# Moving the v loads of an attention and gated scan kernel from SyncE's DMA queue to ScalarE's, with all orders searched anew

## The chip, the core and the metric

The kernel runs on one core of a Trainium2 chip. The metric is the device time in microseconds (us) of one execution, as a median over several runs. A run counts as slow when it is over 1.5% above the fastest run of the same kernel in its group; only fast runs enter the ratios. Several kernels below have runs on both sides of that mark, and this is said where it matters. The kernel before itself straddles it in two groups: with v1, v2 and e4 four of its 7 runs count as slow, with e5, v7 and v2's repeat seven of its 11, most of them at a granted clock of 0.99 to 1.00. Ratios from these groups compare with its fastest runs (fast means 174.6 and 173.9 us), so they come out up to 1% high.

## The reference, cut to what matters

```python
scores = q @ k.T / sqrt(64)              # 8 batches, 8 heads, 576 positions, 64 wide
scores = where(|i - j| <= 32, scores, -1e9)
x = softmax(scores) @ v                  # then heads side by side: 8 x 576 x 512
val, gate = split(x @ w_in)              # 512 -> 2 x 512
h[t] = exp(A_log[0]) * h[t-1] + val[t]   # a scan over the 576 positions
out = (silu(gate) * h) @ w_out           # 512 -> 512, float32
```

Inputs are float32 and are cast on the chip to half precision.

## The kernel before

The order of every engine's work is fixed in advance: one string per engine holds one letter for each operation (`SEQ`), a second table says which engine takes an operation that several could do (`SHARED`), and `ORDER` lists the loads. A small model in the program replays these strings to give out buffers and to merge them into one program.

```python
SLOTS = {"stg": 5, ..., "v32": 2, "vE": 2, "vO": 2, "pr": 3, ..., "f2k": 16, ...}
SEQ = {
    "act": "qexExhxexwhwwxwwxgegEgxhvxTgkTEgwgegqxooxEgovooeoxxETxxEoeogxgTxxgxegEkvgvxxgeEooxxg"
    ...                                  # cut
    "sp": "LLLLLLLLLLLLLLLLLLLLLLLLLLLLLLLLLLLLLLLLLLLLLLLLLLLLLLLLLLLLLLLLOLLOOLLLOLLLLLLLOOOL"
    ...                                  # cut; L is any load, O a store of the output
}
ORDER = ["q01", "a", "q00", "k00", "v01", "v00", "w00", "k01", "k10", "v02", "v03", "q10",
         "v04", "w01", "w02", "w11", "w03", "w12", "w13", "w10", "q11", "k11", "v10", "v11", ...]
...
        if kd == "ld" and key[0] in "qk":          # rows of 9 x 64 floats: 2304 bytes
            nc.sync.dma_start(out=bf(n, b, T).rearrange("p y j d -> p y (j d)"), in_=...)
        elif kd == "ld" and key[0] == "v":         # rows of 64 floats: 256 bytes
            _, b, x = key
            lo = 128 * x - 32
            p0, p1 = max(0, -lo), min(128, S - lo)
            nc.sync.dma_start(out=bf("v32", b)[p0:p1, x],
                              in_=v[b, :, lo + p0:lo + p1, :].rearrange("h p d -> p h d"))
...                                      # cut
        elif kd == "out":
            nc.sync.dma_start(out=out_flat[r0:r0 + 128, :], in_=bf("o", *key))
    idle = keep_busy(seq, place, 45.0)   # filler matmuls in the first 45 us
```

Names as in the profile: v is the float32 buffer of a v load; vE its cast, vO the copy shifted by 64 positions; pr the exponentials; qT, kT the transposed q and k; f2k a buffer that weights, scans and outputs share. A batch has five v loads: three of 128 positions (1024 rows of 256 bytes, 64 for each of 16 DMA engines) and, at its two ends, two of 96 (48 rows each).

The softmax here doesn't subtract the row's maximum and nothing guards it: scores larger than these inputs give would overflow.

Of the kernel before, what the change touches and what calls it, by code (L numbers as in the profile page):

```python
# [22 lines left out]
    ("act", "ev"): (1.012, 1.18), ("act", "exp"): (0.905, 1.09), ("act", "tanh"): (0.48, 0.63),  # L23
# [13 lines left out]
START = {"pe": 0.5, "act": 2.5, "dve": 0.5, "pool": 5.0, "sp": 0.8}  # L37
SWITCH, CAP, DLAT, DPRE = 0.095, 190, 1.75, 0.65
SLOTS = {"stg": 5, "q16": 2, "k16": 2, "qT": 3, "kT": 3, "v32": 2, "vE": 2, "vO": 2, "pr": 3,
         "rc": 2, "x16": 2, "xT": 2, "f2k": 16, "th": 3, "si": 3, "fu": 2}  # L40
LETTER = {"L": "ld", "w": "cw", "a": "ar", "k": "ck", "K": "trk", "E": "evk", "q": "cq", "Q": "trq",
          "e": "evq", "v": "cv", "h": "sh", "m": "mask", "S": "sc", "x": "exp", "P": "pv", "r":
          "rc", "n": "norm", "t": "xt", "T": "xe", "V": "pjv", "G": "pjg", "s": "scan", "g": "tanh",
          "u": "silu", "f": "fuse", "F": "fin", "o": "fev", "O": "out"}

SEQ = {
    "pe": "mQmQKSKKmSPSQPSmtmPSPSVtVGQGKGmSGPPmVStVPPGVKtGVVQGVSSFFFKGQFFQFmmSPSPKPPtSSFtKQVPPF"
          "GVSGtmmSVSPPVGSQtGKPPGVVSSGQKFVFSSPGFPPtGVQtKFGPSSGQKVFFGQVSSFtPPFVQtGKGPPSVGKVGVFFS"
          "SVGtFPPSFQtKVQVSSPGVGGFKFPPPFtVSSSGtFVGVGSPFFVFVPPPVFtGGVGVtGFVGGVFFFFFFF",
    "act": "qexExhxexwhwwxwwxgegEgxhvxTgkTEgwgegqxooxEgovooeoxxETxxEoeogxgTxxgxegEkvgvxxgeEooxxg"  # L50
           "kqogveEogxvxEgqooegxokxeogEgvxgvgEoxxogToxoeEexxgkgoEovgvoTxxgxoggooxoTggoTgogggoooo"
           "oo",
    "dve": "akaEehkhrnqrnETrnrnssTussuhvhurrnnshsrsrnnsussssusussvusmmqehvhurnrnrnrnqTmmrnrsnhhu"
           "ussrrnnsumTurrnnsushhmusrmmnrunrnTTusrnuhmeushsuTrnrnsTmurnusrunshshmsuurrnnmTssmrsu"
           "unrrnnrunhhsTusmsmrnuusmrnsrrnsunussssuusuussso",
    "pool": "aaqvkvvvvmwwwqkvvvfffqfwwwffkvvkffkvvvvvmqffkfqvvvfvqmfffkvfmvfqmffkkvfvvfmqfqmfvfvm"
            "fvfmffffffffff",
    "sp": "LLLLLLLLLLLLLLLLLLLLLLLLLLLLLLLLLLLLLLLLLLLLLLLLLLLLLLLLLLLLLLLLOLLOOLLLOLLLLLLLOOOL"
          "LLLOOLOLOLOOOLOOOOLOOOOOOOOOOOOOOOOOO",
}  # L60
SHARED = {
    "cw": "GAAAAAGGGGGA",
    "ar": "GDGD",
    "ck": "DGDGAGGGGAAGAGGA",
    "evk": "DADAAAAAAAAAAAAA",
    "cq": "AGDGGADDGGAGAGGG",
    "evq": "ADAAADAAAAADAAAA",
    "cv": "GGGGGGGDGADGAGDGGGGGGAAGGGAGAGGAAGGGAGAG",
    "sh": "DDAADDADDDDDDDDDDDDD",
    "mask": "pppGppppDDppDDGppDDDDGDGGDDGGDDGGDDD",  # L70
    "xe": "DDAAADADDDDDADADAA",
    "fev": "AAAAAAAAAAAAAAAAAAAAAAAAAAAAAAAAADAA",
}
ORDER = ["q01", "a", "q00", "k00", "v01", "v00", "w00", "k01", "k10", "v02", "v03", "q10",
         "v04", "w01", "w02", "w11", "w03", "w12", "w13", "w10", "q11", "k11", "v10", "v11",
         "v12", "v13", "v14", "k20", "q20", "v22", "w23", "w22", "w20", "w21", "v20", "q21",
         "k21", "v21", "q30", "v23", "v24", "k30", "k31", "q31", "v30", "v33", "v31", "v32",
         "v34", "v44", "q40", "k41", "k40", "v41", "q41", "v40", "v42", "v43", "q51", "q50",
         "v50", "v51", "k50", "k51", "v52", "v53", "v63", "q60", "v54", "v60", "k60", "q61",
         "v61", "k70", "v62", "k61", "v71", "v64", "q70", "q71", "v73", "v70", "v72", "k71",  # L80
         "v74"]
# [3 lines left out]
def issue(o):  # L85
    return 0.9 if o.kind == "ld" and o.key[0] == "v" else 0.45


def DESC(o):

    return {"v": 48 if o.key[2:] in ((0,), (4,)) else 64, "q": 16, "k": 16, "w": 8, "a": 32}[o.key[0]] if o.kind == "ld" else 8
# [16 lines left out]
def build(order):  # L108
# [15 lines left out]
    g = last.get  # L124
    for it in order:
        if it[0] in "qk":
            add("ld", it, 0, ("sp",), 1.82, (), [("stg", it)])
        elif it[0] == "v":
            _, b, e = it
            add("ld", it, 0, ("sp",), 1.05 if e in (0, 4) else 1.3, (),  # L130
                [("v32", ("v32", b))])
        elif it[0] == "a":
            add("ld", it, 0, ("sp",), 0.8, ())
        else:
            add("ld", it, 0, ("sp",), 0.79, (), [("f2k", ("w32",) + it[1:])])
    for i in range(3):
        for a in range(4):
            add("cw", (i, a), 0.2 * i + 0.05 * a, ("dve", "act", "pool"), "cw", [g(("ld", "w", i, a))], (), [("w32", i, a)])
    for cc in range(4):
        add("ar", (cc,), 0, ("dve", "pool"), "ar", [g(("ld", "a"))])  # L140
    for b in range(B):
        for T in range(2):
            st = step_of(b, T)
            for n in "kq":
                c = add("c" + n, (b, T), st, ("pool", "dve", "act"), "cqk", [g(("ld", n, b, T))],
                        [(n + "16", (n + "16", b, T))], [(n, b, T)])
                t = add("tr" + n, (b, T), st, ("pe",), "tr", [c], [("ps2", ("tr" + n, b, T))], [(n + "16", b, T)])
                add("ev" + n, (b, T), st, ("act", "dve"), "ev", [t], [(n + "T", (n + "T", b))], [("tr" + n, b, T)])
        for e in range(5):
            add("cv", (b, e), step_of(b, 0) + 0.1 * e, ("pool", "act", "dve"), "cv", [g(("ld", "v", b, e))],  # L150
                [("vE", ("vE", b))], [("v32", b)])
        for T in (0, 1) if b < 2 else (2,):
            es = range(4) if T == 2 else range(2 * T, 2 * T + 2)
            for i in range(2):
                add("sh", (b, T, i), step_of(b, 0) + 0.1 * i, ("dve", "act"), "sh" if T == 2 else "sh1",
                    [g(("cv", b, e + i)) for e in es], [("vO", ("vO", b))], [("vE", b)])
# [22 lines left out]
    for c in range(NCH):  # L179
# [18 lines left out]
        for tt in range(4):  # L198
            k, st = (c, tt), 4 * c + tt
            fs = (2 * (tt // 2), 2 * (tt // 2) + 1) if hv else range(4)  # L200
            f = add("fin", k, st, ("pe",), "fin", [g(("fuse", c, x)) for x in fs] + [g(("cw", 2, a)) for a in range(4)],
                    [("ps1", ("fo",) + k)], [("fu", c)])
            e = add("fev", k, st, ("act", "dve") if c == NCH - 1 else ("act",), "fev", [f], [("f2k", ("o",) + k)], [("fo",) + k])
            add("out", k, st, ("sp",), 0.79, [e], (), [("o",) + k])
# [5 lines left out]
def follow():  # L210
# [4 lines left out]
    eng_of = {"p": "pe", "A": "act", "D": "dve", "G": "pool"}  # L215
# [20 lines left out]
    mode, dma, lock, seq, ring = 0, 2.4, 0.0, [], []  # L236
# [4 lines left out]
    while len(seq) < len(ops):  # L241
        best = None
        for e in ENGINES:
            if not todo[e]:
                continue
            o = todo[e][-1]
            if any(d.end is None for d in o.deps):
                continue
            r = max([d.end for d in o.deps] + [0.0])
            for p, k in o.new:  # L250
                if k in held:
                    continue
                if p == "ps1":
                    c = [t for t in bank if t is not None]
                elif p == "ps2":
                    c = [max(bank[b], bank[b + 1]) for b in pairs()]
                else:
                    c = list(free[p].values())
                r = max(r, min(c)) if c else 1e9
            if r > 1e8:  # L260
                continue
            s = max(r, tf[e])
            if e == "pe" and MODE.get(o.kind, 0) != mode:
                s = max(r, tf[e] + SWITCH)
            if best is None or s < best[0]:
                best = (s, e, o)
        s, e, o = best
        todo[e].pop()
        if e == "sp":
            dma = max(dma, s + issue(o) + DPRE) + o.cost  # L270
            o.end = dma + DLAT
            ring.append((dma, o.cost, DESC(o)))
            room, tf[e] = CAP, s + issue(o)
            for end, took, n in reversed(ring):
                if end <= tf[e]:
                    break
                if n > room:
                    tf[e] = max(tf[e], end - room / n * took)
# [70 lines left out]
def kernel(  # L349
# [40 lines left out]

    for tl in bufs["v32"]:
# [47 lines left out]
    def emit(o):  # L439
# [17 lines left out]
        elif kd == "ld" and key[0] == "v":  # L457
            _, b, x = key
            lo = 128 * x - 32
            p0, p1 = max(0, -lo), min(128, S - lo)  # L460
            nc.sync.dma_start(out=bf("v32", b)[p0:p1, x],
                              in_=v[b, :, lo + p0:lo + p1, :].rearrange("h p d -> p h d"))
        elif kd == "ld" and key[0] == "a":
            nc.sync.dma_start(out=a_log, in_=moe_A_log.rearrange("(a p) -> p a", p=128))
            nc.scalar.activation(a1, a_log, AF.Exp, bias=0.0, scale=1.0)
# [142 lines left out]
        elif kd == "out":  # L608
            c, tt = key
            r0 = 512 * c + 128 * tt  # L610
            nc.sync.dma_start(out=out_flat[r0:r0 + 128, :], in_=bf("o", *key))
# [37 lines left out]
```

## Time and profile before

| | before |
|---|---|
| median of the first 3 runs | 175.71 us (175.24 to 176.26) |
| span of the profiled run, granted clock | 174.8 us, 1.00 |
| busy: TensorE, VectorE, ScalarE, GpSimd | 162.5, 144.6, 130.8, 114.9 us |
| first scores, first projection | 15.24, 28.95 us |

The main views are in the prediction below. Four more lines are needed for the comparison. First, section 4 of the page, the chain that ended last, as shares of the span by engine:

```profile
PE 65%; DVE 13%; ACT 8%; POOL 7%; issue 5%; POOLq 0%; ACTq 0%; DVEq 0%
```

No DMA is on this chain. Next, GpSimd's wait for v loads (us in total, times, longest), and how long a v load takes from issue to landing (shortest, median, longest):

```profile
POOL vE L429 <- DMA v<-in_v_dram: 6.5, 4, 2.2
...
DMA to landing us min/median/max: 3.9/7.2/9.0
```

Last, the stretch from 40 to 50 us (length, then busy time of PE, PEld, DVE, ACT, POOL, the granted clock, the DMA share, GB/s):

```profile
40.00:50.00 10.00, 9.96 (x147) 8.80 (x145) 9.50 (x17) 7.75 (x10) 5.67 (x7) 1.00 1.10 322
```

Both TensorE and the DMA engines are full there.

### The profile page before, as it was taken

What the parts mean: (1) busy time and instruction counts of PE and PEld (TensorE: products, weight loads), DVE (VectorE), ACT (ScalarE), POOL (GpSimd) and SP (SyncE); (2) the same over time, 40 slices, a digit from 0 to 9 for tenths busy, and PEclk for the clock granted to TensorE, in tenths of its full rate; (3) what the DMA queues carried; (4) which work ended last, traced back from release to release, by engine and by line L of the source; (5) the groups of instructions that cost most, each with busy time, mean ns of one, the idle gap of its engine ahead of it and who ended that gap; (6) DMA issues with size and microseconds to landing.
All of it is one profiled execution on the core that took longest, in us unless ns stands there. A gap on an engine that the chain in (4) does not pass through costs nothing.

```text
span 174.8 us, 5309 instructions
## 1 busy us (share of the span) xinstructions
PE 162.5 (93%) x2178; PEld 101.8 (58%) x2178; DVE 144.6 (83%) x233; ACT 130.8 (75%) x172; POOL 114.9 (66%) x117
## 2 busy tenths in 40 slices
PE   1996999979999899999999999999999999999991
PEld 0343657848976585565647655654674654558740
DVE  5348467798999989999998899999979699899850
ACT  2232599886699998869999999877998993545552
POOL 7954409672699393499719879885999855505550
PEclk9999999999999999999999999999999999999999
DMA  4999999899999999999999999999950311401155
GB/s 125 293 294 271 313 373 288 162 326 325 329 208 344 226 219 342 270 245 267 264 307 267 325 303 348 262 323 311 353 174 4 120 64 60 161 23 60 64 212 208
DMA packets 53671, 41.23 MB, mean 236 GB/s; under 512 B 39312, under 2 KB 39312, under 8 KB 53648
## 3 DMA queue, kind: packets, MB, share of 16 engines
q1 hardware_dynamic: 53648, 40.90, 81.5%
q8 instruction: 17, 0.28, 0.7%
q14 instruction: 6, 0.05, 0.1%
HBM read 31.46 MB, written 9.44 MB: 234 GB/s over the span
## 4 chain that ended last, share of the span: by engine, by line
PE 65%; DVE 13%; ACT 8%; POOL 7%; issue 5%; POOLq 0%; ACTq 0%; DVEq 0%
PE psum L576 25%; PE psum L604 14%; PE psum L616 7%; PE psum L493 5%; PE psum L546 4%; PE psum L561 4%; PE psum L522 4%; DVE vO L425 3%; DVE si L589 3%; DVE f2k L584 2%; DVE pr L536 2%; ACT pr L527 2%; POOL fu L599 1%; ACT qT L422 1%; POOL pr L536 1%
## 5 line engine op out<-in xcount | busy, mean ns | idle before, releaser
L576 PE MATMUL psum<-xT,w_in 128*128 128x256 f16 (+1 forms) x384 | 69.9, 326 | 0.0
L576 PEld LDWEIGHTS <-w_in 128*128 128x128 f16 x384 | 35.5, 98 | 20.3 <-issue 0.2
L584 DVE TENSOR_TENSOR_SCAN f2k<-arep,f2k,psum 128x512 f32<-128x512 f32 (+1 forms) x44 | 44.4, 1029 | 1.9 <-PE psum L576 1.3
L527 ACT ACTIVATE pr<-psum 128x1024 f16<-128x1024 f32 x36 | 36.5, 1034 | 7.8 <-PE psum L522 7.4
L599 POOL TENSOR_TENSOR fu<-f2k,si 128x512 f16<-128x512 f32 x24 | 30.0, 1255 | 11.2 <-DVE si L589 7.0
L604 PE MATMUL psum<-w_out,fu 128*128 128x512 f16 x144 | 35.1, 379 | 0.1
L536 POOL TENSOR_TENSOR pr<-pr,mask 128x1024 f16<-128x1024 f16 x9 | 20.0, 2219 | 19.3 <-ACT pr L527 19.3
L587 ACT ACTIVATE th<-psum 128x512 f16<-128x512 f32 x36 | 21.8, 604 | 7.0 <-PE psum L576 6.9
L589 DVE SCALAR_TENSOR_TENSOR si<-th,psum 128x512 f16<-128x512 f16 x36 | 24.1, 676 | 3.0 <-ACT th L587 2.8
L422 ACT ACTIVATE f2k<-psum 128x512 f32<-128x512 f32 x35 | 20.8, 612 | 6.9 <-PE psum L604 6.2
L555 DVE TENSOR_TENSOR x<-psum,rc 128x512 f16<-128x512 f32 x36 | 24.1, 683 | 0.6
L596 POOL TENSOR_TENSOR fu<-f2k,si 128x512 f16<-128x512 f32 x12 | 14.8, 1232 | 13.7 <-DVE f2k L584 6.1
L429 POOL TENSOR_SCALAR vE<-v 128x512 f16<-128x512 f32 x27 | 18.2, 687 | 6.5 <-DMA v<-in_v_dram 6.5
L604 PEld LDWEIGHTS <-fu 128*128 128x128 f16 x144 | 13.2, 98 | 13.5 <-issue 0.2
L422 ACT ACTIVATE qT<-psum 128x1152 f16<-128x1152 f16 x13 | 14.8, 1141 | 3.9 <-PE psum L493 3.7
L422 ACT ACTIVATE kT<-psum 128x1152 f16<-128x1152 f16 x14 | 16.0, 1146 | 1.7 <-PE psum L493 1.7
L546 PEld LDWEIGHTS <-pr 128*64 128x64 f16 x576 | 11.4, 111 | 7.1 <-issue 4.5
L522 PEld LDWEIGHTS <-kT 64*128 64x128 f16 x576 | 10.4, 95 | 8.0 <-issue 4.5
L522 PE MATMUL psum<-qT,kT 64*128 64x64 f16 x576 | 13.5, 191 | 1.7 <-DVE kT L425 1.5
L546 PE MATMUL psum<-vO,pr 128*64 128x65 f16 x256 | 13.4, 197 | 1.7 <-DVE vO L425 1.7
L546 PE MATMUL psum<-vE,pr 128*64 128x65 f16 x320 | 14.0, 197 | 0.3 <-DVE pr L536 0.2
L616 PE MATMUL psum<-eye,ident 128*128 128x512 f16 x44 | 13.7, 457 | 0.4 <-ACT pr L527 0.4
(58 smaller groups left out, 198.7 us busy)
## 6 DMA issues: line engine op xcount, KB each, us to landing
stg<-in_q_dram SPq DMA_DIRECT2D x16, 576.0 KB, 7.2
stg<-in_k_dram SPq DMA_DIRECT2D x16, 576.0 KB, 6.6
out_dram<-f2k SPq DMA_DIRECT2D x36, 256.0 KB, 4.2
v<-in_v_dram SPq DMA_DIRECT2D x24, 256.0 KB, 7.4
v<-in_v_dram SPq DMA_DIRECT2D x16, 192.0 KB, 6.9
f2k<-in_moe_w_in_dram SPq DMA_DIRECT2D x8, 256.0 KB, 7.4
f2k<-in_moe_w_out_dram SPq DMA_DIRECT2D x4, 256.0 KB, 7.6
a_log<-in_moe_A_log_dram SPq DMA_DIRECT2D x1, 2.0 KB, 4.2
```

What stands on the lines that cost most here:

```text
L422: nc.scalar.activation(dst, src, AF.Copy, bias=0.0, scale=mul)
L522: nc.tensor.matmul(out=sc[:, h, 256 * t + 64 * r:256 * t + 64 * r + 64], lhsT=kT[64 * h:64 * h + 64, 64 * i:64 * i + 128], rhs=qT[64 * h:6 ...
L527: nc.scalar.activation(bf("pr", *key), bf("sc", *key), AF.Exp, bias=0.0, scale=1.0 / 8.0)
L536: (nc.vector if e == "dve" else nc.gpsimd).tensor_tensor(out=pr, in0=pr, in1=m[:, None, :].to_broadcast([128, 2, 512]), op=ALU.mult)
L546: nc.tensor.matmul(out=pv[p0:p0 + 64, h, x0:x0 + 65], lhsT=pr[:, h, at:at + 64], rhs=vt, start=True, stop=True)
L555: nc.vector.tensor_tensor(out=x, in0=view[:, :, :, 0:64], in1=bf("rc", *key)[:, :, :, None].to_broadcast([128, 2, 4, 64]), op=ALU.mult)
L576: nc.tensor.matmul(out=to, lhsT=w_in16[:, fc, 128 * w:128 * w + 128], rhs=xT[:, fc, t0:t0 + n], start=(fc == 0), stop=(fc == 3))
L584: nc.vector.tensor_tensor_scan(out=bf("h", c, x)[:, lo:lo + n], data0=arep[:, cc, a0:a0 + n], data1=bf("pjv", c, x)[:, lo:lo + n], initial ...
L589: nc.vector.scalar_tensor_tensor(out=bf("si", *key), in0=bf("th", *key), scalar=1.0, in1=bf("pjg", *key), op0=ALU.add, op1=ALU.mult)
L599: eng.tensor_tensor(out=bf("fu", c)[:, x, :], in0=bf("h", *key), in1=bf("si", *key), op=ALU.mult)
L604: nc.tensor.matmul(out=fo, lhsT=fu[:, cc, 128 * tt:128 * tt + 128], rhs=w_out16[:, cc, :], start=(cc == 0), stop=(cc == 3))
L616: nc.tensor.matmul(out=psum[:, bank, :], lhsT=ident, rhs=eye8.rearrange("p r q -> p (r q)"), start=True, stop=True)
```

## The change

The intent: v loads have short rows and long issues, and they hold up the other loads in SyncE's queue. They go to ScalarE's queue, half of the stores follow, and all orders are searched anew with a model that knows of eight transfers in flight over both queues. The core of the diff:

```diff
-    "act": "qexExhxexwhwwxwwxgegEgxhvxTgkTEgwgegqxooxEgovooeoxxETxxEoeogxgTxxgxegEkvgvxxgeEooxxg"
+    "act": "blllAllvvvxExqlxxlleETTllxEvxxwxggghgklgElewgxxllwlelvglgooEloolxoxloxxTlooveElgxxxl"
...                          # all strings are new; l is a v load, O a store
-ORDER = ["q01", "a", "q00", "k00", "v01", "v00", "w00", "k01", "k10", "v02", "v03", "q10", ...
+ORDER = ["a", "q00", "k00", "k01", "q01", "q10", "k10", "w01", "w00", "q11", "w02", "w03",
+         "k11", "w10", "w12", "w11", "w13", "k21", "k20", "w20", "q20", "q21", "w23", "q30", ...
...
+            if o.kind in MOVES and len(moves) >= AFOOT:      # AFOOT = 8
+                r = max(r, moves[-AFOOT])
...
-            nc.sync.dma_start(out=bf("v32", b)[p0:p1, x],
-                              in_=v[b, :, lo + p0:lo + p1, :].rearrange("h p d -> p h d"))
+            nc.scalar.dma_start(out=bf("v32", b)[p0:p1, x],
+                                in_=v[b, :, lo + p0:lo + p1, :].rearrange("h p d -> p h d"))
...
+        elif kd == "tb":
+            nc.scalar.activation(a1, a1, AF.Exp, bias=0.0, scale=1.0)
...
-            nc.sync.dma_start(out=out_flat[r0:r0 + 128, :], in_=bf("o", *key))
+            (nc.sync if e == "sp" else nc.scalar).dma_start(out=out_flat[r0:r0 + 128, :], in_=bf("o", *key))
```

## The prediction

> **What bounds the kernel now.** I read the slices of the page first, then the chain that ended last, then the DMA queue's own timeline and waits, then the busy time by stretch. Slices of the page (40 slices of 4.37 us, busy share in tenths):
>
> ```profile
> PE   1996999979999899999999999999999999999991
> DVE  5348467798999989999998899999979699899850
> ACT  2232599886699998869999999877998993545552
> DMA  4999999899999999999999999999950311401155
> ```
>
> TensorE looks full from the second slice on, and so do the 16 DMA engines until 125 us. TensorE's early part is not work, though. From the chain of waits in order of time (start, length, what), L616 being matmuls on the identity that only keep the clock up (fillers):
>
> ```profile
> 5.18 6.15 PE psum L616 x15
> ...
> 13.05 0.68 PE psum L493 x9
> 13.83 1.37 DVE kT L425
> 15.24 0.41 PE psum L522 x16
> 15.65 2.27 PE psum L616 x10
> ...
> 18.42 1.08 PE psum L616 x5
> ...
> 21.67 1.46 PE psum L616 x6
> ...
> 26.15 1.19 PE psum L616 x5
> ...
> 28.97 1.01 PE psum L576 x8
> ```
>
> The first scores (L522) come at 15.24, the first projection (L576) at 28.97. Fillers on the chain before that are 6.15 + 2.27 + 1.08 + 1.46 + 1.19 = 12.15 us.
>
> How much work TensorE really has, by the pace that the chain shows where nothing is waited for: 192 projection matmuls of 512 columns at 0.86/4 us = 41.3; 192 of 256 columns at 3.49/32 = 20.9; 144 output matmuls at 0.86/4 = 31.0; 32 groups of 9 transposes at 0.50 = 16.0; 18 groups of 8 at 0.45 = 8.1; 36 score groups at 0.34 = 12.2; 36 value groups at 0.37 = 13.3; 11 mask pairs at 0.32 = 3.5. Sum 146.3 us. From its first matmul on the chain (4.58) to its last (171.2) there are 166.6 us, so 20.3 are lost. Up to 28.97 its order holds 6 transpose groups, 6 scores, 4 values, 5 masks, 1 of L561: 3.0 + 2.0 + 1.5 + 1.6 + 0.45 = 8.6 us of work in 24.4 us, so **15.8 of the 20.3 lost us lie before 29 us**. What is left, 4.5 us in 142, can't be cut much: in the stretches 90 to 125 and 125 to 171.3, with sum and busy time of each engine,
>
> ```profile
> 90.00:125.00 35.00, 35.00 (x474) 20.70 (x474) 32.76 (x49) 31.55 (x44) 28.61 (x23) 1.00 1.05 306
> 125.00:171.30 46.30, 46.12 (x530) 27.65 (x524) 38.47 (x60) 31.40 (x47) 28.60 (x23) 1.00 0.30 109
> ```
>
> TensorE (second number) is busy throughout, VectorE (fourth) 94% in the first of them. So the loads bound the first 29 us, TensorE the rest.
>
> Why the loads are late: the timeline of the issuing queue (start, length of the issue itself),
>
> ```profile
> 3.52 1.45 SPq L461 DMA_DIRECT2D v<-in_v_dram  x2
> 5.01 3.60 SPq L472 DMA_DIRECT2D f2k<-in_moe_w_in_dram  x1
> 8.65 1.34 SPq L455 DMA_DIRECT2D stg<-in_k_dram  x2
> 10.04 2.31 SPq L461 DMA_DIRECT2D v<-in_v_dram  x2
> 12.47 3.27 SPq L455 DMA_DIRECT2D stg<-in_q_dram  x1
> 15.79 0.60 SPq L461 DMA_DIRECT2D v<-in_v_dram  x1
> 16.43 3.83 SPq L472 DMA_DIRECT2D f2k<-in_moe_w_in_dram  x7
> ```
>
> A free issue takes about 0.6 us (7 in 3.83). The one at 5.01 takes 3.60 and that at 12.47 takes 3.27, each behind v loads, whose rows are 256 bytes and so need many descriptors: the queue's room is full. And its waits in the first 30 us hold transfers that it doesn't need (line waited for: total, times, longest):
>
> ```profile
> SPq L461 <- DMA f2k<-in_moe_w_in_dram: 2.1, 3, 1.4
> SPq L472 <- DMA stg<-in_q_dram: 0.6, 1, 0.6
> ```
>
> Those are waits for an earlier transfer's landing, not for a buffer: the limit on transfers in flight.
>
> **What the Trainium skill says.** "DMA: Bandwidth & Descriptors", section "Issuing engines are not separate DMA queues": a second issuing engine uses the same 16 DMA engines and saves only issue time. The trace agrees that there is no bandwidth to find: the DMA share is 1.02 to 1.07 in all stretches from 4 to 125 us. I therefore count no faster transfers. Same page, "Queues, rings and completion order": each DMA engine takes turns between the queue rows packet by packet. Before has only one row (q1) in use, so nothing here shows it. "Perfetto Trace Analysis", section "Per-instruction lifecycle: what the profiler-reported window actually captures": an ACT instruction is pushed into a wait queue and the sequencer goes on, while a DMA instruction holds the sequencer from its wait to the end of its issue. So issues may hide behind activations, waits can not. No run so far shows a DMA on ACT. "ScalarE: Activation LUTs", section "What ACT_TABLE_LOAD costs": about 1.28 us; the trace has 1283 ns, once, beginning at 0.80; the new dummy exponential doesn't add one.
>
> **The change part by part.**
> (1) 40 v loads leave SyncE's queue. Its long issues go (3.60 + 3.27, less 1.2 for two free ones, 5.7 us of issue time in the first 16 us). As the DMA engines were fed meanwhile, that is not 5.7 us of gain: it is a better order of arrival.
> (2) New order: a, q00, k00, k01, q01, q10, k10, then weights; before had q01 ahead of q00. Rates from the DMA view of the first 34 us: q alone runs near 410 GB/s, so 589,824 bytes take 1.44 us; v alone near 190, so 262,144 bytes take 1.38 and 196,608 take 1.03. k00 arrived at 9.84 (VectorE's cast starts then). One q transfer fewer lies ahead of it and up to one v beside it: about 8.5 to 9.5. Cast 1.18, transposes 0.68, two evictions of 1.36 on VectorE: first scores at about 13.5 instead of 15.24.
> (3) The first projection needs w00 to w03. By the new order the engines have then moved: start 2.3, a_log 0.75, 7 q/k at 1.44 = 10.1, 4 quarters at 0.64 = 2.6, batch 0's v at 2 x 1.03 + 3 x 1.38 = 6.2; together 21.9. Landing about 1.2, cast 0.63: 23.7. TensorE's order must also have done its attention, so I take **25 instead of 28.97: 4.0 us**. Up to there the new order holds 7 transpose groups, 5 scores, 4 values, 6 masks, 2 of L561: 9.5 us of work against 8.6, 0.9 more done.
> (4) 15 mask pairs on TensorE instead of 11: 4 x 0.32 = 1.3 us more work on the bound.
> (5) ScalarE gives away 5 casts of q/k (5.9), 3 of weights (1.9), one eviction each of q and k (2.3), 2 output copies (1.2), one shift (1.1), and takes 2 v casts (1.3): 11 us less than 130.8. It takes 58 DMA issues: at 0.5 us each 29 us of its sequencer, at worst 120 + 29 = 149 of 172. Most should lie behind activations.
> (6) VectorE: 5 v casts, 1 weight cast, 2 evictions, 2 output copies, 1 shift more; 2 q/k casts and 3 masks fewer: about +3 us on 144.6. GpSimd about +3 on 114.9. Both have their slack in the first 40 us.
> (7) Tail: half of the output stores on ScalarE. After the last copy (ends 171.88) the rest is one store either way: 0.
>
> Sum: 175.7 - 4.0 - 0.9 + 1.3 = 172.1; I say **172.0**.
>
> **The rivals.**
> A, ScalarE becomes the bound: a v load that waits for its buffer, for queue room or for the eighth transfer back blocks exponentials, tanh and copies behind it. For it: ScalarE is 15.58 of 16 us busy from 46 to 62, VectorE nearly as much, with in-order queues any slip spreads. Against: 11 us were cleared and the orders were made for these waits. If half the issues' 29 us show and a quarter of that reaches TensorE, 3 to 4 us: 175.5.
> B, the load was hidden anyway: TensorE merely swaps fillers for waiting, because the fixed amount of data (weights and two batches) is what counts, and the DMA engines were already full. Then only the earlier first scores (1.7) stay, less the masks: 175.
> C, two rows overlap what one can't (many small packets of one beside large ones of the other), so the loads up to 40 us run some 8% faster: 3 us more, 169.
> D, turn-taking by packet starves v beside q/k: the first values wait, VectorE's order puts a v shift before k's eviction. 175 to 178.
>
> **Range and chances.** A and B pull up 3 us, C pulls down 3, D is less likely. 168.8 to 175.5 for 8 in 10. The border of 2% is 172.2, just above my number: faster 0.50, same 0.43, slower 0.07.
>
> **What would show it.** Right: first scores near 13.5, first projection near 25, fillers before it about 8 us instead of 12, TensorE full from 29 us on, ScalarE busy about 120. Wrong: the first projection still after 27.5 (B or D), or TensorE gaps of over 0.5 us after 40 us that end with an activation whose queue was in a v issue (A), or GB/s clearly above 300 in the first 40 us (C).

## The result

The changed kernel took **189.89 us** (median of 4 runs, 189.06 to 191.95) beside 175.99 us before (median of 4, 175.24 to 176.42), 13.9 us more. The ratio is 1.078, 95% interval 1.070 to 1.086. Here and below a ratio is the mean time of one kernel's fast runs over that of the other's fast runs of the same rounds, so it isn't quite the ratio of the medians quoted.

The slices of the page after (40 slices of 4.68 us, busy share in tenths; PEclk is the granted clock in tenths):

```profile
PE   1989479579999999949999889999999999999991
...
ACT  3218407085888879938887699885787957647341
...
PEclk9999957988999999999999999999999999999999
DMA  5999999990449999991898899978691220140065
```

TensorE, nearly full before from the second slice on, now has holes in slices 5, 6, 8 and 9 and again in slice 18. The DMA engines, without a pause before until slice 30, stand idle in slice 10, over half idle in 11 and 12, and idle once more in slice 19. The granted clock falls too, in slices 6 to 10. The chain that ended last:

```profile
PE 46%; DMA 25%; DVE 14%; issue 4%; ACT 4%; ACTq 4%; DVEq 0%
```

A quarter of it is now waiting for transfers. In order of time (start, length, what):

```profile
0.98 3.47 DMA v<-in_v_dram
...
4.47 17.73 DMA v<-in_v_dram
...
22.22 4.38 DMA f2k<-in_moe_w_in_dram
...
26.62 7.04 DMA f2k<-in_moe_w_out_dram
...
33.68 3.22 ACTq L461
...
66.56 14.29 DMA v<-in_v_dram
```

One v load takes **17.73 us**; four weights of w_in are issued within 0.02 us of its landing. A second late v load, 14.29 us, stands on the chain from 66.56 on, just before the hole in slice 18. SyncE doesn't use v, yet its own queue waits for v in two groups of lines (us in total, times, longest):

```profile
SPq L475 <- DMA v<-in_v_dram: 15.9, 4, 5.3
...
SPq L455 <- DMA v<-in_v_dram: 5.3, 3, 3.7
```

That is the limit on transfers in flight: a new one waits for an old one of the other queue. Those four weights were issued from 22.22 on; in the kernel before, seven of the eight were issued between 16.43 and 20.26. GpSimd's wait for v and the landing times, to be set beside those of before:

```profile
POOL vE L429 <- DMA v<-in_v_dram: 25.1, 6, 11.5
...
DMA to landing us min/median/max: 2.7/5.6/17.7
```

The median got better (7.2 to 5.6), the longest twice as long. Why one v load takes so long is seen in the DMA view, for 8 to 12 us, with both queues at work (packets, MB, share of 16 engines; q1 is SyncE's queue, q10 ScalarE's):

```profile
q1 hardware_dynamic: 599, 1.30, 90.2%
q10 hardware_dynamic: 589, 0.15, 18.4%
```

The two queues moved **equal numbers of rows**, not of bytes: nearly nine times as many bytes went to q and k. From 12 to 16 us it was 567 and 718 rows, from 16 to 20 us 647 and 649. The sum fits the landing: batch 0's v has 288 rows per DMA engine, 4608 in all; the view counts 1438 on q10 up to 4.5 us, 3104 up to 20 and 146 up to 22.2, together 4688. The 80 more are 16 for each of the five loads: the page's total on q10, 40096, is likewise 36864 rows of v, 2304 of the stores and 16 for each of its 58 transfers. Equal turns are no strict rule: from 4.5 to 8 us q10 moved 1148 rows beside 381.

The second half of the mechanism is in the timeline (start, length, and in brackets the idle time before it and what ended it):

```profile
27.73 1.13 ACT L422 ACTIVATE qT<-psum 128x1152 f16<-128x1152 f16 x1 [6.04 <-DVE x L558]
...
32.06 4.83 ACTq L461 DMA_DIRECT2D v<-in_v_dram  x2
36.99 1.02 ACT L530 ACTIVATE pr<-psum 128x1024 f16<-128x1024 f32 x1 [5.10 <-issue]
...
42.81 0.62 POOL L429 TENSOR_SCALAR vE<-v 128x512 f16<-128x512 f32 x1 [11.51 <-DMA v<-in_v_dram]
```

This reads as a ring. Batch 0's last v lands at 22.2, so x is late, so ScalarE stands 6.04 us before qT. Batch 1's last v loads come after that in ScalarE's order. The pair at 32.06 takes 4.83 us in all: 0.38 us for the first issue, then a wait until 33.68, when a w_out load has just landed (26.62 + 7.04 on the chain above, so the limit holds ScalarE too), then 3.22 us for the second issue. An earlier pair at 3.55 (4.76 us) had one issue of 3.84 us; most v issues on this queue take about 0.4. I read the two long ones as the queue's room being full; no run measures that room. The exponential after the second pair waits 5.10 us for it. The last of batch 1's v arrives for GpSimd at 42.81, after 11.51 us of standing still; GpSimd meanwhile frees no buffers (SyncE's queue waits 8.5 us for its next cast of k), and the loads stop. Two stretches of the changed kernel, columns as above:

```profile
25.00:30.00 5.00, 4.79 (x51) 3.48 (x46) 4.57 (x9) 2.19 (x3) 4.94 (x7) 0.50 1.01 356
...
40.00:50.00 10.00, 9.83 (x142) 7.43 (x140) 8.76 (x16) 7.89 (x11) 4.30 (x5) 0.83 0.24 65
```

From 40 to 50 us the DMA share is 0.24, against 1.10 before. After TensorE's idle stretch from 20 to 25 us (1.33 us busy) the granted clock is 0.50, so the 4.79 busy us held at most about half of that in work. That idleness lowered the clock is argued here, not tested.

How far behind this puts the kernel: counting the matmuls of each group that have begun, and weighing them by the pace that the prediction lists, I estimate 23.5 us of useful TensorE work done by 46 us in the kernel before and 18.3 in the changed one (85 projection matmuls against 50); by 125 us 100.5 and 90.0. Of the 12.5 us by which the span grew, some 5 thus lie before 46 us and as much again between 46 and 125, where the second late load is. Which loads carry the loss is asked in e3 and e4.

### The profile page after: what moved, and what is told of

Read it like the earlier page. It is cut to its first block, busy times and chain, and to the rows that moved or that the text cites. A ratio compares the mean times of both kernels' runs of the same rounds, so it can differ in the third digit from the quotient of the medians.

```text
span 187.3 us, 5285 instructions
## 1 busy us (share of the span) xinstructions
PE 164.8 (88%) x2175; PEld 102.7 (55%) x2175; DVE 152.3 (81%) x240; ACT 124.2 (66%) x162; POOL 117.1 (63%) x118
## 3 DMA queue, kind: packets, MB, share of 16 engines
q10 hardware_dynamic: 40096, 14.16, 30.7%
## 4 chain that ended last, share of the span: by engine, by line
PE 46%; DMA 25%; DVE 14%; issue 4%; ACT 4%; ACTq 4%; DVEq 0%
PE psum L579 22%; DMA v<-in_v_dram 19%; PE psum L607 11%; PE psum L496 4%; DVE f2k L587 4%; DMA f2k<-in_moe_w_out_dram 4%; PE psum L549 4%; ACTq L461 3%; PE psum L525 3%; DVE vO L425 2%; DMA f2k<-in_moe_w_in_dram 2%; PE psum L564 2%; DVE vE L425 2%; DVE si L592 2%; DVE x L558 1%
## 5 line engine op out<-in xcount | busy, mean ns | idle before, releaser
L530 ACT ACTIVATE pr<-psum 128x1024 f16<-128x1024 f32 x36 | 36.1, 1024 | 13.6 <-PE psum L525 6.3
L429 POOL TENSOR_SCALAR vE<-v 128x512 f16<-128x512 f32 x20 | 13.9, 701 | 25.1 <-DMA v<-in_v_dram 25.1
L422 ACT ACTIVATE f2k<-psum 128x512 f32<-128x512 f32 x33 | 19.5, 600 | 11.0 <-PE psum L607 10.9
L539 POOL TENSOR_TENSOR pr<-pr,mask 128x1024 f16<-128x1024 f16 x8 | 17.5, 2188 | 12.6 <-ACT pr L530 12.6
L549 PE MATMUL psum<-vO,pr 128*64 128x65 f16 x256 | 14.7, 202 | 7.0 <-DVE vO L425 6.5
L425 DVE COPY vO<-vE 64x2080 f16<-64x2080 f16 (+1 forms) x18 | 14.4, 800 | 6.4 <-POOL vE L429 3.2
L422 ACT ACTIVATE qT<-psum 128x1152 f16<-128x1152 f16 x12 | 13.4, 1131 | 7.5 <-DVE x L558 6.0
L429 POOL TENSOR_SCALAR k<-stg 128x1152 f16<-128x1152 f32 x13 | 16.2, 1251 | 3.0 <-DMA stg<-in_k_dram 2.8
L422 ACT ACTIVATE kT<-psum 128x1152 f16<-128x1152 f16 x13 | 14.7, 1128 | 3.7 <-DMA v<-in_v_dram 1.9
L549 PE MATMUL psum<-vE,pr 128*64 128x65 f16 x320 | 15.1, 203 | 0.8 <-ACT pr L530 0.3
L429 POOL TENSOR_SCALAR q<-stg 128x1152 f16<-128x1152 f32 x12 | 13.8, 1151 | 2.3 <-DMA stg<-in_q_dram 1.6
```

The costliest lines, as they stand in the source:

```text
L422: nc.scalar.activation(dst, src, AF.Copy, bias=0.0, scale=mul)
L425: nc.vector.tensor_copy(dst, src)
L429: nc.gpsimd.tensor_scalar(out=dst, in0=src, scalar1=mul, scalar2=1.0, op0=ALU.mult, op1=ALU.mult)
L530: nc.scalar.activation(bf("pr", *key), bf("sc", *key), AF.Exp, bias=0.0, scale=1.0 / 8.0)
L549: nc.tensor.matmul(out=pv[p0:p0 + 64, h, x0:x0 + 65], lhsT=pr[:, h, at:at + 64], rhs=vt, start=True, stop=True)
```

## The experiments

The theory: v's short rows, sharing the DMA engines row for row with long ones, arrive late (S); this then blocks ScalarE through its queue's room and SyncE through the limit. The rivals: the new orders are bad by themselves (O); the stores on ScalarE (T); and, named B in the expectations, issuing alone blocks ScalarE, whether or not v lands late (the prediction's rival A, not its B). B is the one that these runs don't separate from S. The kernels differ from the one named in the lines shown. "First projection" is when the first projection matmul starts in the profiled run.

| kernel | v loads on ScalarE's queue | median, range, runs (us) | ratio to before | first projection | longest v landing |
|---|---|---|---|---|---|
| before | none | 175.99 | | 28.95 | 9.0 |
| changed | all | 189.89, 189.06 to 191.95, 4 | 1.078 [1.070, 1.086] | 31.28 | 17.7 |
| e1 | none | 176.8, 173.9 to 179.49, 4 | 0.996 [0.979, 1.014] | 25.79 | 9.8 |
| e2 (old orders) | all | 194.25, 192.96 to 194.46, 4 | 1.104 [1.094, 1.113] | 40.36 | 12.6 |
| e3 | batches 2 to 7 | 178.38, 177.69 to 179.08, 2 | 1.015 [1.001, 1.030] | 25.07 | 13.7 |
| e4 | batches 0 and 1 | 185.53, 184.97 to 186.1, 2 | 1.064 [1.031, 1.097] | 32.22 | 18.9 |
| v1 | fourth and fifth of each batch | 178.88, 177.99 to 180.42, 4 | 1.028 [1.005, 1.051] | 27.36 | 12.2 |
| v2, first time | fifth of each batch | 174.83, 173.48 to 175.1, 4 | 1.001 [0.987, 1.016] | 25.81 | 10.0 |
| v2, again | the same | 175.89, 174.75 to 176.83, 6 | 1.010 [1.002, 1.019] | 25.83 | 11.0 |
| v7 (old orders) | fifth of each batch | 175.86, 175.54 to 182.3, 4 | 1.011 [1.001, 1.020] | 28.46 | 11.1 |

### e1: the new orders, v back on SyncE's queue

```diff
-            nc.scalar.dma_start(out=bf("v32", b)[p0:p1, x],
+            nc.sync.dma_start(out=bf("v32", b)[p0:p1, x],
```

> The changed kernel with its v loads back on SyncE's queue, all orders kept. Theory S (two queues take turns row by row, so v's 256-byte rows starve beside q and k's 2304-byte rows): no v load lands later than 10 us after its issue (17.7 in the changed kernel), the DMA engines' idle stretch of 40 to 48 us goes, time 171 to 178 us. Theory B (ScalarE is blocked by issuing): the same time, so this run alone does not tell S from B. Theory O (the new orders are bad, wherever v is issued): stays above 184 us.

176.8 us: the whole loss is gone, with orders and stores as in the changed kernel. The longest landing is back at 9.8 us, and the DMA engines no longer stop between 40 and 48 us. So the queue that v is on makes the loss, not the orders (O) and not the stores (T), which are on ScalarE here too. S and B both expected this, so the run does not tell them apart. It isn't a gain either, though the first projection starts 3.2 us before that of the kernel before. Two of its four runs are slow, the profiled one among them (span 177.8, clock 0.98), so its times by stretch are not set against those of before. A fast profile of the same kernel is x5's, below: there GpSimd's last cast of batch 0's v begins at 17.48 us, in the changed kernel at 22.35, and the first projection at 26.64 against 31.28. x5 first, then the changed kernel:

```profile
17.48 0.62 POOL L429 TENSOR_SCALAR vE<-v 128x512 f16<-128x512 f32 x1 [0.22 <-DMA v<-in_v_dram]
...
22.35 0.62 POOL L429 TENSOR_SCALAR vE<-v 128x512 f16<-128x512 f32 x1 [4.23 <-DMA v<-in_v_dram]
```

The 4.9 us by which v comes later cover the 4.6 us by which the projection does.

### e2: the kernel before, v on ScalarE's queue

```diff
-            nc.sync.dma_start(out=bf("v32", b)[p0:p1, x],
+            nc.scalar.dma_start(out=bf("v32", b)[p0:p1, x],
```

> The kernel before with nothing changed but the queue of its v loads, ScalarE's instead of SyncE's. S: longest v landing over 14 us (9.0 in before), rows of both queues in equal number where both are full, time 182 to 200 us. B: slower too, but v lands as in before (at most 9 or 10 us) and ScalarE idles on issues for 10 us or more. O: within 2% of 176 us.

194.25 us, 18 more than before, so the move costs with the old orders too. The longest landing is 12.6 us, between what S (over 14) and B (at most 9 or 10) expected, and ScalarE stands 5.8 and 2.5 us before activations with its queue in v issues, where B expected 10 us or more: here both look at work. The DMA view of its profile from 11 to 12.5 us shows the equal rows in another kernel, though only for that stretch (from 9 to 10 us it is 170 rows on q1 and 13 on q10):

```profile
q1 hardware_dynamic: 240, 0.52, 88.7%
q10 hardware_dynamic: 238, 0.06, 17.9%
```

The new orders thus win back some 4 us of what the move costs (194.25 to 189.89).

### e3 and e4: the first two batches alone, and all others alone

```diff
 e3
-            nc.scalar.dma_start(out=bf("v32", b)[p0:p1, x],
+            (nc.sync if b < 2 else nc.scalar).dma_start(out=bf("v32", b)[p0:p1, x],
 e4
+            (nc.scalar if b < 2 else nc.sync).dma_start(out=bf("v32", b)[p0:p1, x],
```

> The changed kernel with the v loads of the first two batches on SyncE, the other 30 on ScalarE. S: the waits on v before 45 us go (the first projection at 25 to 28 us instead of 31.3), but a v landing of 12 us or more stays later on: 177 to 184 us. If only the start-up counts: 171 to 176 us. O: above 184 us.

> The changed kernel with the v loads of batches 2 to 7 back on SyncE, those of the first two on ScalarE: the complement of the run that had the first two on SyncE (178.4 us). If the start-up holds nearly all of the loss: first projection at 31 us as in the changed kernel, 185 to 190 us. If the loss is spread over the kernel: 180 to 184 us.

With only batches 0 and 1 on ScalarE's queue the time is 185.53, with only the other six 178.38. The first two batches carry most of the loss. The chain of e4 has the same piece in it as that of the changed kernel (start, length):

```profile
4.33 18.88 DMA v<-in_v_dram
```

### e5: all stores back on SyncE's queue

```diff
-            (nc.sync if e == "sp" else nc.scalar).dma_start(out=out_flat[r0:r0 + 128, :], in_=bf("o", *key))
+            nc.sync.dma_start(out=out_flat[r0:r0 + 128, :], in_=bf("o", *key))
```

> The changed kernel with all 36 output stores on SyncE's queue, v still on ScalarE's: the other part of the change undone alone. If the stores on ScalarE cost (issues ahead of its copies) or gain nothing much: 188 to 191 us as the changed kernel. If they were what blocks ScalarE: below 186 us.

186.45 (fast) and 191.51 (slow): the fast run lies 3.2 us below the fast mean of the changed kernel (189.62), between the two ranges expected, and a landing of 18.8 us remains. T is not the cause, as e1 shows as well; whether the stores cost 3 us or nothing, one fast run is too few to say.

### e6: v loads marked as single packets

```diff
-                                in_=v[b, :, lo + p0:lo + p1, :].rearrange("h p d -> p h d"))
+                                in_=v[b, :, lo + p0:lo + p1, :].rearrange("h p d -> p h d"), single_packet=True)
```

> The changed kernel with each v load marked as a single packet, so that a turn should move the 64 rows that one DMA engine has of it; same queue, same orders, same waits. S: longest v landing under 10 us, ScalarE's long issues (4.76 and 4.83 us) shrink as the queue drains, time 170 to 178 us. B: ScalarE still issues 40 loads, so it stays above 184 us. O: above 184 us. If the mark does nothing, v's longest landing stays near 17 us and the run tells nothing.

189.38 us, ratio 1.078, and from 8 to 12 us 598 and 596 rows: nothing changed, the counts are still equal. The mark did not do what I had hoped, so this run tells nothing for or against S.

### m1 and m2: the transfers by themselves

Both move data only (a wrong result). m1 issues two v-like loads of 1024 short rows on ScalarE's queue beside six q-like loads on SyncE's; m2 first lets five long loads into the other queue, then issues three short ones:

```python
# m1: (a, "short"), (s, "long"), (a, "short"), 5 * (s, "long")     a: ScalarE's queue, s: SyncE's
# m2: 5 * (s, "long"), then (a, "short"), (a, "short"), (a, "short")
```

> A kernel that only moves data (its result is wrong on purpose), to measure the disputed cost by itself, in phases that wait for one another, each twice: two v-like loads (64 rows of 256 bytes on each DMA engine) alone on ScalarE's queue; the same beside six q-like loads (16 rows of 2304 bytes) on SyncE's; the same beside three loads of 256-byte rows on SyncE's; and two v-like loads ahead of six q-like ones, all on SyncE's. If the queues take turns row by row, at some 0.114 us for a pair of a long and a short row (2560 bytes at the 358 GB/s of the changed kernel's trace): alone 3.6 and 5 us from issue to landing; beside long rows 9.5 and 13.8; beside short rows 5 and 7.7; ahead on one queue 3.6 and 5. If they take turns by bytes or by whole transfers: beside long rows no more than 5 and 8 us, the same as beside short rows.

> Again only data movement (result wrong on purpose), closer to the changed kernel's state than the first one, where v came first: five q-like loads on SyncE's queue alone; the same five with three v-like loads issued on ScalarE's queue some 2.4 us later, when the long rows are queued deep; the three alone; two beside two loads of rows as short. If the engines take turns row by row: the first v-like load needs 64 turns of 0.114 us, so 9 to 10 us from issue to landing against 3.6 alone, while rows of both queues pass in equal number; beside short rows about 5 us. If they take turns by whole transfers, as parts of the first measurement look: 5 to 6.5 us, and the counts of rows in half a microsecond swing between the queues.

In m1 the first short load landed after 3.2 and 3.1 us in the two repetitions, as alone, the second after 8.6 and 5.6, where 9.5 and 13.8 were expected: row-by-row turns as a rule for the time missed here. The v rows came first and the shares swing, as they did from 4.5 to 8 us in the changed kernel. But m1 has a control, the same loads all on SyncE's queue with the two short ones ahead: they landed after 3.2 to 3.3 and 3.8 us. So the second queue by itself delayed the second load, by 4.8 and 1.8 us. The lines of the first repetition (KB of each, median us from issue to landing), first on two queues, then on one:

```profile
besidexshort_t<-in_v_dram ACTq DMA_DIRECT2D x2, 256.0 KB, 5.9
...
onexshort_t<-in_v_dram SPq DMA_DIRECT2D x2, 256.0 KB, 3.6
```

In m2 the long loads are ahead. The page's DMA issues (columns as above), first the short loads alone, then behind long ones:

```profile
alonexshort_t<-in_v_dram ACTq DMA_DIRECT2D x3, 256.0 KB, 3.9
...
behindxshort_t<-in_v_dram ACTq DMA_DIRECT2D x3, 256.0 KB, 9.3
```

3.9 against 9.3 us for the same bytes; the first of the three took 8.6 and 8.9 in the two repetitions. For 3.4 us after the issue no short row moves at all (alone the first moves within 1.5), then rows come in equal numbers (from 26.5 us on 85 and 66, 77 and 72, 67 and 70 in half-microseconds). The third issue took 4.74 us on ScalarE. So the delay and the long issue both appear with no compute in the program. What m2 does not show is that one queue would have been better for these loads: only 249 short rows of 3072 moved by 28 us, the rest after the long loads were nearly done, and no phase puts the short ones behind the long ones in one queue.

### v1, v2 and v7: only some of v on ScalarE's queue

```diff
 v1 (from the changed kernel)
+            (nc.sync if x < 3 else nc.scalar).dma_start(out=bf("v32", b)[p0:p1, x],
 v2 (from the changed kernel) and v7 (from the kernel before)
+            (nc.sync if x < 4 else nc.scalar).dma_start(out=bf("v32", b)[p0:p1, x],
```

> The changed kernel with three of each batch's five v loads on SyncE and the last two on ScalarE. If the mixture of two queues is what moves more bytes in a second (355 against 284 GB/s) and starvation only hurts loads that are needed soon, the engines finish the loads some 5 us sooner and the first projection comes at 24 to 26 us: 170 to 174 us. If any v load on ScalarE that lands late stops the casts behind it: a landing over 10 us, 176 to 182 us.

> As the one above, with only the last of the five v loads on ScalarE (48 rows on each DMA engine). Starvation rule: it lands within 48 turns, about 5.5 us and a latency of 2, so none over 10 us: 171 to 175 us. If two queues cost something in themselves: 177 or more.

> The version with only the last v load of each batch on ScalarE's queue, once more with more rounds, to see whether it beats the kernel before: it was at 174.83 us against 176.07 us. If the gain at the start (first projection 3.1 us sooner) is kept to the end: 172.5 to 174.0 us, ratio about 0.985. If it is given back: 174.5 to 176, ratio 0.99 to 1.00.

> The kernel before with only the last v load of each batch moved to ScalarE's queue, its orders kept. If two queues help as long as the moved load is not needed soon: 173 to 175.5 us. If the orders have to be made for it (its last v load of batch 0 is wanted early, and ScalarE's orders have no room for issues): 176.5 to 181 us.

The cost grows with the share of v that is moved: 189.9 with all, 178.9 with two fifths of the loads, about 175 with one fifth. v2 looked like a gain of a microsecond in its first group; with five rounds its median is 175.89 beside 175.66 and its ratio 1.010 (against the low fast mean of 173.9), so it is none. v7's 175.86 lies in neither range expected. No mixture beat the kernel before.

### x1 to x5: where the earlier start goes

e1 and v2 start the first projection some 3 us sooner and end no sooner. The theory was that the later loads become the bound between 46 and 125 us: in the profile of v2's second group GpSimd waits 4.0 us for v there, where before shows no wait for a load. x1 and x3 take e1's kernel and cut the v loads of batches 3 to 7 to four heads of eight and to one (wrong); x2 and x4 do the same to the kernel before; x5 is e1's kernel again, as the control of x3 and x4 on one chip.

```diff
-            nc.sync.dma_start(out=bf("v32", b)[p0:p1, x],
-                              in_=v[b, :, lo + p0:lo + p1, :].rearrange("h p d -> p h d"))
+            n = 8 if b < 3 else 4           # x3, x4: 1
+            nc.sync.dma_start(out=bf("v32", b)[p0:p1, x, 0:n],
+                              in_=v[b, 0:n, lo + p0:lo + p1, :].rearrange("h p d -> p h d"))
```

> The new orders with v on SyncE's queue (as in e1), and the v loads of batches 3 to 7 cut to four of the eight heads (the other heads reuse older values: a wrong result on purpose). Theory (the loads become the bound between 46 and 125 us once the start is faster): at most 173 us, 3 us or more below e1's 176.8, and the waits of Pool and VectorE for v after 46 us, together 5.8 us in e1, fall below 2. Rival (TensorE, VectorE or the orders themselves bind there): within 1 us of e1, 175.8 to 177.8.

> The kernel before with the same cut of v's loads from batch 3 on (wrong on purpose). Both accounts: no wait for a load between 46 and 125 us is there to take away, so within 1 us of the kernel before, 175 to 177 us; if it falls by 3 us as well, the cut helps in some way other than by the waits of the new orders, and the first run doesn't count for the theory.

> The kernel of e1 once more (the new orders, v on SyncE's queue, nothing cut), as the control on the same chip for the two that follow. 175 to 177 us, within 1% of the kernel before.

> The new orders with v on SyncE's queue, v's loads of batches 3 to 7 cut to one of eight heads (wrong on purpose). Theory (late loads take back the start's gain in the middle): at least 2 us below the uncut control on the same chip, about 173.5, as the lead at 46 us of some 3 to 4 us, less 1.3 us for the added mask products, then stays. Rival (loads don't matter there; TensorE, VectorE and the orders take the lead back): within 1 us of the control.

> The kernel before with the same cut (wrong on purpose). Both accounts: within 1 us of the kernel before, since nothing in it waits for a load between 46 and 125 us. A fall as large as that of the new orders would speak against the theory.

| kernel | median, range, runs (us) | mean of fast runs | ratio to before |
|---|---|---|---|
| x1, new orders, half of v | 174.23, 173.58 to 175.12, 4 | 174.29 (4) | 0.996 [0.988, 1.004] |
| x2, before, half of v | 175.64, 175.61 to 175.67, 4 | 175.64 (4) | 1.004 [0.995, 1.012] |
| x5, new orders, all of v | 177.09, 174.29 to 178.57, 6 | 175.07 (3) | 0.997 [0.991, 1.004] |
| x3, new orders, an eighth of v | 174.97, 173.35 to 176.38, 6 | 174.64 (5) | 0.994 [0.988, 0.9995] |
| x4, before, an eighth of v | 175.71, 174.68 to 176.73, 6 | 175.66 (6) | 1.001 [0.996, 1.006] |

x1's 174.23 lies in neither range expected (at most 173, or 175.8 to 177.8); by fast runs it is 0.8 us below e1 (175.11), so within the rival's 1 us, and GpSimd still waits 3.4 us for v after 46 us where the theory expected under 2. For the larger cut, the medians would favour the theory (177.09 to 174.97), but three of x5's six runs, at 178.07 to 178.57, are slow, one of them with a clock of 0.999. By the fast runs the large cut is worth 175.07 - 174.64 = 0.43 us, within the 1 us that the rival had allowed. x5's profiled run speaks against the theory as well. It is a fast one, 174.29 us, and its waits from 46 to 125 us hold this line:

```profile
POOL vE L429 <- DMA v<-in_v_dram: 7.0, 3, 4.1
```

That is more waiting for v than in v2's profile, in a run of its fast group. So **late loads are not shown to take the start's gain back**. That theory falls for the fast runs. That half of the uncut kernel's ten runs (e1 and x5) lie at 177.29 us or above, and none of the ten of x1 and x3 above 176.4, is a difference that only slow runs show, and it is left unexplained.

What the pairs with equal cuts do allow is an account of the lead. By 46 us x1 has an estimated 27.2 us of useful TensorE work done and x2 24.4, x3 has 26.3 and x4 23.5 (counted as above, one profile each): a lead of 2.8 us in both pairs. The new orders also put four more mask pairs on TensorE, by the prediction's working 1.3 us. That leaves 1.5 us; measured at the end are 175.64 - 174.29 = 1.35 and 175.66 - 174.64 = 1.02 us. So in these pairs most of the lead is paid for masks or arrives. In the uncut kernel only 0.3 to 0.4% arrives, and the interval doesn't exclude zero.

## Why the prediction was wrong

The step that failed is the premise behind parts (1), (2) and (3), "it is a better order of arrival": that with v on its own queue batch 0's v comes in early, so that only a weight's landing and cast and a little attention stand between the sum of 21.9 us and the first projection. The sum itself held: w00 to w03 had landed by 23.05 (the last issued at 17.45, landing 5.6 us later), where 21.9 + 1.2 = 23.1 were predicted. The order in it did not. With two queues, a load of many short rows beside long ones got about as many rows through as they did and so a small part of the bytes (599 and 589 rows with 1.30 and 0.15 MB in 4 us). So batch 0's last v took 17.73 us, where 9.0 was the longest, and came at 22.2, hardly sooner than the weights; the attention that needs it took until 31.28 (26.64 in x5, where v was in by 17.48). The sum also has no term for the limit that the two queues share, which only rival A names ("the eighth transfer back") and which then held the next weights and batch 1's v.

- **Bound.** The reading of before held: in its first 29 us the arrival of data is what counts. That is why a change of arrival could cost as much: e3 and e4 put most of the loss into the first two batches. The claim that TensorE alone binds from 29 us on did not carry over to the changed kernel, which lost some 5 us more between 46 and 125 us.
- **(1) v leaves SyncE's queue.** Its two long issues went, but SyncE got waits of 15.9 and 5.3 us for v's landing in their place. Wrong: the limit is common to both queues, and the lateness of v passes to the weights.
- **(2) First scores.** They came at 14.43, not 13.5; before 15.24. Right in direction, half in size.
- **(3) First projection at 25.** 31.28, past the 27.5 that the prediction had set as its sign of being wrong (B or D). With v on SyncE's queue the same orders have it at 25.79 and 26.64 (e1, x5): the orders do what they were made for if transfers arrive in order.
- **(4) Masks.** Not measured by themselves; the account of x1 to x4 is consistent with 1.3 us (2.8 us of lead, 1.35 and 1.02 at the end).
- **(5) ScalarE.** Its busy time fell to 124.2, not to 119.8. What mattered was the issues: "Most should lie behind activations" failed in two places early on, with single issues of 3.84 and 3.22 us and ScalarE idle for 4.62 and 5.10. That is rival A's mechanism, though its sign was set for gaps after 40 us.
- **(6) VectorE and GpSimd.** VectorE's busy time is 152.3 against 147.6 expected, GpSimd's 117.1 against 117.9; neither sets the time.
- **(7) Tail.** e5 gives no sign that the stores matter much.
- **The rivals.** D, turn-taking by packet, happened and drew A after it; D was called "less likely" and put at 178 at most, 2 us above the kernel before, where with all that followed, rival A's part included, it cost 13.9. I had the rule that would have told me, but "Before has only one row (q1) in use" was taken as a reason to set it aside. C did occur in part: from 4.5 to 20 us 5.43 MB moved against 4.52 before, but with fewer packets under 512 bytes among them (3246 against 5252), so this is no proof of a faster path. The prediction's B is not what e1 shows: the start does come sooner.
- **The last step, a sooner start is a sooner end.** Even with arrival in order, the sum of 3.6 us gained became 0.3 to 0.4% (0.6 us), too little to tell from none. Part of that is the size of the start's gain (2.3 to 3.2 us, where 4.0 were taken) and the masks; for the rest no cause is shown.

Open: how the 13.9 us split among late v (S), ScalarE's blocked queue (B of the expectations), the limit and the lower clock, since no run removes one of them alone (e6 was meant to and did not); why the shares swing where short rows come first, and why the short rows of m2 and e2 wait over 3 us before their first turn; and what keeps the new orders from a gain.

## What to carry to other kernels

Before a stream of loads moves to a second queue, compare its row length with that of the stream it will meet: where the two streams move row for row, as in the stretches above, its time is set by its number of rows and not by its bytes. The number of rows per DMA engine times the time of one row of each is an estimate for a load behind long ones (9 to 10 us expected in m2, 8.6 and 8.9 measured), too high for one ahead of them (13.8 expected in m1, 8.6 and 5.6 measured). Work this out for the load that compute waits for first, and follow a late landing through every shared limit (transfers in flight, queue room, in-order issue) to the loads of the other queue. Where a sooner start has to become a sooner end, measure that step too.

## What the Trainium skill lacked or had wrong

- "DMA: Bandwidth & Descriptors", "Queues, rings and completion order" has the turn-taking by packet, and the equal counts agree (599 and 589 rows, 647 and 649), though they don't show how many rows a turn takes. It lacks what follows for bytes: 1.30 against 0.15 MB, and 17.73 us for one v load of 192 KB. Nor are the counts always equal: 1148 beside 381 from 4.5 to 8 us, and none beside q1's 611 in m2 from 22.0 to 25.5.
- The same page, "Issuing engines are not separate DMA queues" says that transfers of several issuing engines interleave, and that a second one only saves issue time. It lacks that the move can cost: e2 became 10.4% slower by it. Nor was the issue time always saved: 4.74 us for the third issue in m2, 3.84 and 3.22 for single ones in the changed kernel.
- "Perfetto Trace Analysis", "DMA Optimizations" says that spreading DMAs over the issuing engines may help where descriptor generation is the bottleneck. SyncE's issues of 3.60 and 3.27 us looked like that case; a caution about short rows beside long ones is missing (nothing but the queue of v was changed in e2).
- No page that I read says what marking a load as a single packet does to the turns; in e6 the counts stayed at 598 and 596.
